# Tiles 10 and 11 of the second FFN layer as a seventh pair of seven block products, with the engines' lists laid out anew from batch 3's loads on

## The chip, the cores and the metric

The kernel runs on one core of a Trainium2 chip, which has five engines with an instruction list each: TensorE (PE, with its weight loads shown apart as PEld), VectorE (DVE), ScalarE (ACT), GpSimd (POOL) and SyncE (SP). They wait for each other through semaphores alone. The metric is the device time of one execution in microseconds, the median of several runs.

## The reference

Block-sorted attention for 4 batches of 8 heads (768 tokens, head size 64, blocks of 96 tokens), then a feed-forward network (FFN) over the 3072 tokens that come out. Cut to what matters:

```python
P = sinkhorn(sort_net, rounds=5)                  # 8x8 per batch and head
k_sorted = einsum('bhij,bhjcd->bhicd', P, k_b)    # and v_sorted alike
scores = q_b @ k_sorted.T / sqrt(64)              # within a block of 96
attn = softmax(scores); x = attn @ v_sorted       # x: 3072 tokens x 512
h = x @ w_in                                      # 512 x 2048
g = maximum(h, 0) + alpha * minimum(h, 0)
out = g @ w_out                                   # 2048 x 512
```

## The kernel before

**Stages.** One batch's attention and the FFN of the tokens that came out earlier run interleaved. A group g = 0..31 is one block of 96 tokens over 8 heads. For a group of batches 1 to 3, `attention` makes the scores on PE (line 761, into the PSUM tile psS), their negated maxima on DVE (767), eight exponentials on ACT (795), a transposing DMA on SP (800), the product with the sorted v on PE (815, into psO), a reciprocal and a scaling (823, 828, the latter on DVE or ACT), and a transpose into xT (a DMA at 843, or PE and a copy in batch 1). The next group's scores need psS free, which it is when the eight exponentials have read it. `conv_k`, `prep_k`, `conv_v` and `prep_v` sort k and v of the batch ahead: POOL copies (661, 411), PE products (674, 715), and a copy out of PSUM by ACT or DVE (411).

**FFN.** The tokens go in ten chunks, most of 384 tokens. For each of 16 slices of the hidden size `ffn1` makes four matmuls of 384 columns into one of two banks of psH (886), ACT takes the negated positive part (896), and DVE combines the two into hT (900). A psH bank is used again two slices later, so PE waits for line 900 when DVE is late. `ffn2` computes 128 tokens x 512 outputs as 16 matmuls of 512 columns in four groups of four (925), copies them out (411) and stores them (939). Tiles 12 to 23 go in six pairs instead, through `strassen`: the two tiles, each split by even and odd hidden slices, and w_out, split by the halves of its 512 outputs, are 2x2 blocks, and the product takes seven block products in place of eight (the Winograd form). A block product is eight matmuls of 256 columns in two groups of four (1024). It needs eight sums of hidden blocks per pair (999, on DVE or POOL, in the tile Sm or VDz), eight sums of weight blocks that are made once (`w_sums`, 963, in KS, VST and WT), three copies of a partial result to SBUF (`snap`, 1034, listed as line 411) and three additions on DVE on the way out (`total`, 1039).

**What sets the order.** Every piece of work is an entry of a graph, numbered as it is added, with its readers and writers. The table `SEQ` lists the numbers in one order for all engines; a letter behind a number names the engine where the work may run on several (p POOL, a ACT, d DVE). `arrange` splits it into one list for each engine and `emit` writes the lists with the waits that the data need. An engine works its list off in order, so an instruction that waits holds up all behind it. `PAIRS` names the pairs and which of two buffer sets each takes; set 0 is Sm and sn, set 1 VDz and KSz, which `conv_v` and `conv_k` use until batch 3 is sorted. For pairs below 12 the code at 973 and 1004 (`one`) puts all seven products into one PSUM bank, one half of psYP, in another order.

Of the kernel before, what the change touches and what calls it, by code (L numbers as in the profile page):

```python
# [57 lines left out]
712 743 716 736 725 713 720 804 663 717 707 664 721 665d 726 758 710 737 722 744 718 759 639 808 734 698 745
719 610 760 699 666 700d 749 708 735d 740 732 750 746 741 751 733 793 742 747 738 622 613 794 755 739 761 727
611 756 752 728 729d 701 781 768 753 757 795 754 782 805 730 767 775 769 803 776 778 770d 796 828 777 771 762  # L60
606 779 772 607 783 773 787 780 693 829 608 774 790 788 763 612 806 764d 789 797 791 765 807d 784 609 792 830
798 838 785d 810 836 813 811 831 856 837 822 799d 812 840 814 841 748 816 817 842 815 857 839 819 820 864 823
818 844 640 843 667 904p 865d 867 858 868 866 832 821 845 731 847 869d 824 833 846 870 850 848 851 849 853 825
834d 854 859 835 871d 890 852 905p 855 912p 702 826 891 913 872 881 873 882 914p 875 892 874 860 883 861 884
885 862d 887 876 948 888 886 889 898 800 915p 899 949 906p 863 901 900 877 902 878 903 916p 917p 945 942 950
922 946 943 893 968 908 910 947 951 879 959 944 956 969 918p 960 919p 961 957 958 920 921 894 923 965 895 896d
909p 924d 925 962 970 966 926 967 911p 786 897 963 964 988 979 976 971 952 928 880 927 980 989 766 981 977 827
990 907p 978 932d 985 982 929 933 1024p 991 983 953 1008 986 954d 972 984 996 997 987 999 1000 934 955 1009
801 930 973 998 974d 931 1022p 935 1001 1002 1010 992 936 1003 975 1030 937 993 1005 1023p 1031 994d 1004 1058
1034d 1006 938 1007 939 1059 995 1016 1019 1017 940 1018 1020 1036 1032 1021 1033 1052 1035 1011 1025p 1060  # L70
1055 1038 1026p 1027p 1053 1039 1056 1054 1057 1078 1079 1012 1066 1069 1037 1061 1067 1092p 1068 1040 1013
1070 1028p 1072 1071 1042d 1094p 1075 1073 1076 1043 941 1014d 1096p 1044 1097p 1062 1074 1041 1086 1077 1080
1089 1087 1015 1045d 1100 1063 1128 1064d 1029 1101 1090 1104 1088 1091 1122 1046 1125 1129 1065 1048 1093p
1123 1126 1106 1107 1124 1127 1098p 1049 1130 1050 1136 1112 1139 1137 1081 1154 1138 1102 1082 1113 1083 1103
1142 1140 1141 1155p 1114 1143 1105 1145 1146 1108 1144 1148 1156 1147 1109 1095p 1115d 1151 1110 1149 1150
1184 1162 1131 1152 1185 1163 1099 1153 1084d 1186 1188 1166 1157p 1187 1132 1111 1192 1168 1189 1193 1158
1190 1191 1196 1116 1197 1118 1194 1133 1159p 1195 1198 1134 1169 1199 1174d 1119 1161p 1216p 1200 1120 1201
1204 1205 1160 1164 1051 1085 1202 1135 1047 1232 1175 1217p 1165 1203 1206 1207 1176 1167 1208 1212 1177d
1170 1209 1171 1172 1210 1211 1246 1213 1214 1215 1250 1222p 1121 1247 1248 1173 1251 1249 1224 1218p 1225
1228 1252 1254 1255 1220p 1253 1117 1178 1256 1221p 1258 1257 1180 1230 1233 1259 1262 1263 1260 1261 1181  # L80
1266 1223p 1264 1265 1234 1267 1268 1231 1294 1278p 1269 1179 1270 1182 1271 1274 1280p 1286 1275 1272 1226
1227 1273 1276 1236 1235 1277 1279p 1287 1290 1183 1237 1295 1282 1283 1292 1284p 1229 1293 1281p 1238 1296
# [233 lines left out]
def bass_sinkhorn_attn__then__act_prelu_kernel(  # L316
# [634 lines left out]
    def w_sums():  # L951
        w = lambda ft, h: AP(w_out_bf, ft * DM + h * 256, [[FT_TILES * DM, 128], [2 * DM, 4], [1, 256]])
        old = [("KS", 0)], [("VST", 0)] + [("VST", 0, x) for x in range(4)]
        for n, x, y, op in ((1, (0, 1), (0, 0), AluOpType.subtract), (3, (1, 1), (0, 1), AluOpType.subtract),
                            (2, (1, 1), 1, AluOpType.subtract), (4, (1, 0), 2, AluOpType.subtract)):
            for hf in range(2):
                def f(e, n=n, x=x, y=y, hf=hf, op=op):
                    def at(v):
                        if isinstance(v, tuple):
                            return w(8 * hf + v[0], v[1])  # L960
                        t, ld, off = wt(v, 4 * hf)
                        return AP(t, off, [[ld, 128], [256, 4], [1, 256]])
                    return e.tensor_tensor(out=at(n), in0=at(x), in1=at(y), op=op)
# [156 lines left out]
    for t0, t1_, _ in CHUNKS:  # L1120
# [18 lines left out]
    for g in range(NG + 12):  # L1139
        while fp < len(ffn_plan) and ffn_plan[fp][0] < g:  # L1140
# [100 lines left out]
```

## Time and profile before

| | |
|---|---|
| median of 3 runs | 231.47 us (231.02 to 232.26) |
| profiled execution | 231.12 us |
| its span, first to last instruction | 229.4 us |
| TensorE clock granted | 1.000 |
| busy, of the span | PE 95%, DVE 80%, ACT 68%, POOL 68% |

The span is 1.72 us shorter than the time of its execution. Busy shares are means over the whole span, and what decides is which engine the others wait for in the stretch that the change touches. That stretch begins at about 97 us, and its core lies between 107 and 155 us, where tiles 10 and 11 are computed.

### The profile page before, as it was taken

What the parts mean: (1) busy time and instruction counts of PE and PEld (TensorE: products, weight loads), DVE (VectorE), ACT (ScalarE), POOL (GpSimd) and SP (SyncE); (2) the same over time, 40 slices, a digit from 0 to 9 for tenths busy, and PEclk for the clock granted to TensorE, in tenths of its full rate; (3) what the DMA queues carried; (4) which work ended last, traced back from release to release, by engine and by line L of the source; (5) the groups of instructions that cost most, each with busy time, mean ns of one, the idle gap of its engine ahead of it and who ended that gap; (6) DMA issues with size and microseconds to landing.
All of it is one profiled execution on the core that took longest, in us unless ns stands there. A gap on an engine that the chain in (4) does not pass through costs nothing.

```text
span 229.4 us, 6744 instructions
## 1 busy us (share of the span) xinstructions
PE 218.5 (95%) x2717; PEld 151.6 (66%) x2735; DVE 183.2 (80%) x390; ACT 155.4 (68%) x424; POOL 156.8 (68%) x185
## 2 busy tenths in 40 slices
PE   3899999999999999999999999999999999999994
PEld 3457588695556655565565566556777777999983
DVE  5669599896898979777678798899897887886583
ACT  4479667889989595857898787777666673554310
POOL 7969129849075995872989979579965945448760
PEclk9999999999999999999999999999999999999999
DMA  5999999995994499599949998533764223041104
GB/s 64 215 211 202 218 204 190 179 170 91 181 174 86 52 124 115 109 101 251 175 103 110 167 134 153 87 69 91 165 132 82 73 54 80 20 148 49 52 0 184
DMA packets 64031, 29.03 MB, mean 127 GB/s; under 512 B 55280, under 2 KB 58880, under 8 KB 64000
## 3 DMA queue, kind: packets, MB, share of 16 engines
q0 software_dynamic: 24816, 13.63, 46.7%
q1 hardware_dynamic: 39184, 14.97, 32.8%
q8 instruction: 21, 0.34, 0.6%
q14 instruction: 10, 0.08, 0.1%
HBM read 27.28 MB, written 6.29 MB: 146 GB/s over the span
## 4 chain that ended last, share of the span: by engine, by line
PE 75%; DMA 10%; POOL 9%; DVE 3%; issue 1%; ACT 0%; POOLq 0%
PE psH L886 33%; PE psYP L925 16%; PE psYP L1024 12%; DMA KS<-in_k_dram 10%; POOL KSz L661 3%; PE psS L761 3%; PE psO L815 3%; PE psYP L715 3%; PE psO L1024 2%; PE psYP L674 2%; POOL w_in_bf L1102 1%; DVE hT L900 1%; DVE Sm L999 1%; POOL QN L441 1%; PE psS L1024 1%
## 5 line engine op out<-in xcount | busy, mean ns | idle before, releaser
L886 PE MATMUL psH<-xT,w_in_bf 128*128 128x384 bf16 (+1 forms) x624 | 97.3, 295 | 0.5 <-DVE hT L900 0.4
L900 DVE SCALAR_TENSOR_TENSOR hT<-t,omaT,psH 128x384 bf16<-128x384 f32 (+1 forms) x156 | 79.0, 529 | 17.6 <-ACT t L896 16.2
L896 ACT ACTIVATE t<-psH 128x384 f32<-128x384 f32 x126 | 61.2, 495 | 39.5 <-PE psH L886 38.8
L886 PEld LDWEIGHTS psH<-xT,w_in_bf 128*128 128x128 bf16 x624 | 54.5, 98 | 22.1 <-DVE hT L900 1.3
L795 ACT ACTIVATE Esb<-psS,nf 96x96 bf16<-96x96 f32 x192 | 46.1, 344 | 1.1 <-DVE nf L767 1.1
L925 PE MATMUL psYP<-w_out_bf,hT 128*128 128x512 bf16 x174 | 44.8, 379 | 1.3 <-issue 0.5
L411 POOL COPY VDz<-VST 64x384 bf16<-64x384 bf16 x40 | 33.9, 846 | 17.5 <-PE psYP L715 13.1
L661 POOL COPY KSz<-KS 64x512 bf16<-64x512 bf16 x36 | 22.1, 613 | 15.1 <-DMA KS<-in_k_dram 9.0
L925 PEld LDWEIGHTS psYP<-w_out_bf,hT 128*128 128x128 bf16 x192 | 16.9, 98 | 15.4
L767 DVE TENSOR_REDUCE nf<-psS 96x8 f32<-96x768 f32 x24 | 22.8, 948 | 4.3 <-PE psS L761 4.3
L999 POOL TENSOR_TENSOR VDz<-hT 128x512 bf16<-128x512 bf16 x12 | 14.2, 1184 | 9.1 <-DVE hT L900 6.2
L828 DVE TENSOR_TENSOR xq<-psO,rec 96x512 bf16<-96x512 f32 x29 | 19.8, 683 | 0.6
L441 POOL DMA_DIRECT2D QN<-in_q_dram x24 | 20.1, 852 | 0.1
L815 PEld LDWEIGHTS psO<-VS,ET 112*128 112x128 bf16 x248 | 11.0, 98 | 2.7 <-ACT xT L411 0.5
L815 PE MATMUL psO<-VS,ET 112*128 112x65 bf16 x248 | 12.7, 194 | 0.0
L999 POOL TENSOR_TENSOR Sm<-hT 128x512 bf16<-128x512 bf16 x7 | 8.1, 1154 | 6.4 <-DVE hT L900 5.6
L761 PEld LDWEIGHTS psS<-KT,QTz 64*128 64x128 bf16 (+1 forms) x248 | 6.4, 97 | 8.2 <-ACT t L896 3.4
L999 POOL TENSOR_TENSOR Sm<-Sm,hT 128x512 bf16<-128x512 bf16 x5 | 5.8, 1154 | 8.5 <-DVE Sm L999 8.2
L1024 PE MATMUL psYP<-w_out_bf,hT 128*128 128x256 bf16 x80 | 11.2, 273 | 0.0
L761 PE MATMUL psS<-KT,QTz 64*128 64x96 bf16 (+1 forms) x248 | 10.8, 206 | 0.4 <-DVE KT L411 0.4
L411 ACT ACTIVATE VS<-psYP 112x512 bf16<-112x512 f32 x13 | 9.0, 692 | 3.1 <-PE psYP L715 2.8
L411 DVE CAST VS<-psYP 112x512 bf16<-112x512 f32 x13 | 9.0, 690 | 1.8 <-PE psYP L715 1.8
(196 smaller groups left out, 329.3 us busy)
## 6 DMA issues: line engine op xcount, KB each, us to landing
out_dram<-outstg SPq DMA_DIRECT2D x24, 256.0 KB, 2.4
KS<-in_k_dram POOLq DMA_DIRECT2D x3, 768.0 KB, 9.6
QN<-in_q_dram POOLq DMA_DIRECT2D x24, 96.0 KB, 4.9
w_in_bf<-in_moe_w_in_dram POOLq DMA_DIRECT2D x4, 512.0 KB, 18.8
w_out_bf<-in_moe_w_out_dram POOLq DMA_DIRECT2D x2, 1024.0 KB, 19.8
VST<-in_v_dram POOLq DMA_DIRECT2D x4, 384.0 KB, 11.3
hT<-in_q_dram POOLq DMA_DIRECT2D x1, 768.0 KB, 7.3
VST<-in_v_dram POOLq DMA_DIRECT2D x1, 768.0 KB, 13.3
```

Source lines behind the costliest of these rows:

```text
L411: return e.activation(o, i, ACTF.Copy) if e is nc.scalar else e.tensor_copy(o, i)
L661: G.add(POOL, lambda e, hp=hp: e.tensor_copy(AP(KSz, hp * 64 * 3072 + u % 3 * 1024 + hp * 64, [[3072, 64], [128, 8], [1, 64]]), AP(KS[n], ...
L761: inst = e.matmul(o, AP(QTz[n], hp * 64 * 3072 + h4 * 768 + i * 96, [[3072, 64], [1, w]]), AP(KT[n], hp * 64 * ld + (h4 * 8 + i) * bk, [[l ...
L767: G.add(DVE, lambda e: e.tensor_reduce(AP(nx, 0, [[8, 96], [4, 2], [1, 4]]), AP(psX, 0, [[1024, 96], [512, 2], [96, 4], [1, 96]]), AxisLis ...
L795: inst = e.activation(AP(Esb[me], p * 128, [[1024, 96], [64, 2], [1, 48]]), AP(psX, (p // 4) * 512 + (p % 4) * 96, [[1024, 96], [48, 2], [ ...
L815: inst = e.matmul(AP(psZ, hp * 512 + h4 * 68, [[1024, 128], [1, 65]]), AP(ET[me] if far else ET[m], pos(h4, hp) * 96, [[800, nk], [1, 128] ...
L886: inst = e.matmul(AP(pt, poff + x * n, [[1024, 128], [1, n]]), AP(w_in_bf, kt * DFF + (ft + x) * 128, [[KT_TILES * DFF, 128], [1, 128]]), ...
L896: G.add(ACT, lambda e: e.activation(AP(t1, tb, [[1152, 128], [1, k * n]]), AP(pt, poff, [[1024, 128], [1, k * n]]), ACTF.Relu, scale=-1.0) ...
L900: G.add(DVE, lambda e, x=x: e.scalar_tensor_tensor(out=AP(hT, (ft + x) * RING + place(tok), [[FT_TILES * RING, 128], [1, n]]), in0=AP(t1, ...
L925: inst = e.matmul(AP(bank[0], bank[1], [[1024, 128], [1, n]]), AP(hT, ft * RING + place(tok), [[FT_TILES * RING, 128], [1, 128]]), AP(w_ou ...
L999: return e.tensor_tensor(out=sv(n, hf), in0=i[0], in1=i[1], op=op)
L1024: inst = e.matmul(AP(pt, po + off, [[1024, 128], [1, 256]]), sa, mb, start=begin and j == 0, stop=j == 7, skip_group_check=True)
```

## The change

`PAIRS` gains the entry 10, so that tiles 10 and 11 go through `strassen` with buffer set 0 and one PSUM bank. Since the smallest pair is now 10, the weight sums are added to the graph ahead of it, and all later numbers shift. `SEQ` is new from entry 626 on. No other line differs.

```diff
@@ SEQ @@
-626 591 593 556 627 594 600 557 620 625 595 602 628 629 601 621 558d 489 598 596 630 647 597d 599 509 631 559
+626 591 489 625 594 556 627 593 629 595 557 630 558d 628 631 596 620 559 600 597 509 365 560 601 632 621 633
...
-    PAIRS = {12: 1, 14: 0, 16: 1, 18: 0, 20: 1, 22: 0}
+    PAIRS = {10: 0, 12: 1, 14: 0, 16: 1, 18: 0, 20: 1, 22: 0}
```

Counted over the lists, PE loses 32 matmuls of 512 columns and gains 56 of 256. The sums of hidden blocks go from 10 on DVE and 38 on POOL to 20 and 36, and the sums of weight blocks from 2 on DVE and 6 on POOL to 6 and 2. DVE also gains three additions of line 1039 and loses four copies into KT, which ACT takes; ACT gains three copies into sn and one scaling of line 834.

**TensorE, where tiles 10 and 11 end.** Names: psH is written by the first layer, psYP by the second, psS by the scores, psO by attention's second product. Before:

```order
L925 MATMUL psYP<-w_out_bf,hT 128x512 x4
L761 MATMUL psS<-KT,QTz 128x96 x8
L886 MATMUL psH<-xT,w_in_bf 128x384 x8
L925 MATMUL psYP<-w_out_bf,hT 128x512 x4
L815 MATMUL psO<-VS,ET 128x65 x8
L886 MATMUL psH<-xT,w_in_bf 128x384 x8
L925 MATMUL psYP<-w_out_bf,hT 128x512 x4
L761 MATMUL psS<-KT,QTz 128x96 x8
L886 MATMUL psH<-xT,w_in_bf 128x384 x8
L925 MATMUL psYP<-w_out_bf,hT 128x512 x8
```

The same place now:

```order
L761 MATMUL psS<-KT,QTz 128x96 x8
L886 MATMUL psH<-xT,w_in_bf 128x384 x4
L815 MATMUL psO<-VS,ET 128x65 x8
L1024 MATMUL psYP<-VST,Sm 128x256 x8
L886 MATMUL psH<-xT,w_in_bf 128x384 x8
L1024 MATMUL psYP<-WT,Sm 128x256 x4
L761 MATMUL psS<-KT,QTz 128x96 x8
L1024 MATMUL psYP<-WT,Sm 128x256 x4
L886 MATMUL psH<-xT,w_in_bf 128x384 x4
L1024 MATMUL psYP<-w_out_bf,hT 128x256 x12
```

Groups of 512 columns have become groups of 256 that read the sums in Sm, WT and VST, and two score products (line 761) that follow each other have less work between them.

**VectorE, in the middle of the chunk of tokens 1536 to 1919.** hT is the first layer's result, KT the sorted k, nf the negated maxima, rec and xq the scaling of attention. Before:

```order
L900 SCALAR_TENSOR_TENSOR hT<-t,omaT,psH 128x384
L411 CAST KT<-psYP 128x32x2x8
L823 RECIPROCAL rec<-psO 96x8
L900 SCALAR_TENSOR_TENSOR hT<-t,omaT,psH 128x384 x2
L828 TENSOR_TENSOR xq<-psO,rec 96x512
L411 CAST KT<-psYP 128x32x2x8
L900 SCALAR_TENSOR_TENSOR hT<-t,omaT,psH 128x384 x2
L767 TENSOR_REDUCE nf<-psS 96x8
L999 TENSOR_TENSOR VDz<-VDz,hT 128x512
```

The same place now:

```order
L900 SCALAR_TENSOR_TENSOR hT<-t,omaT,psH 128x384 x2
L963 TENSOR_TENSOR VST<-w_out_bf,KS 128x1024
L900 SCALAR_TENSOR_TENSOR hT<-t,omaT,psH 128x384
L999 TENSOR_TENSOR Sm<-Sm,hT 128x512
L823 RECIPROCAL rec<-psO 96x8
L900 SCALAR_TENSOR_TENSOR hT<-t,omaT,psH 128x384
L828 TENSOR_TENSOR xq<-psO,rec 96x512
L900 SCALAR_TENSOR_TENSOR hT<-t,omaT,psH 128x384
L999 TENSOR_TENSOR Sm<-hT 128x512
L767 TENSOR_REDUCE nf<-psS 96x8
```

The copies into KT have gone to ACT, and a weight sum and two hidden sums stand between the first layer's combinations, the last of them ahead of a reduction that the exponentials wait for.

**GpSimd, at batch 3's loads.** VST and KS receive v and k, VDz and KSz their reordered copies. Before:

```order
L475 DMA VST<-in_v_dram 64x1536
L459 DMA KS<-in_k_dram 128x768
L475 DMA VST<-in_v_dram 64x1536 x3
L459 DMA KS<-in_k_dram 128x768 x3
L411 COPY VDz<-VST 64x8x48 x6
L661 COPY KSz<-KS 64x8x64
L411 COPY VDz<-VST 64x8x48 x2
```

The same place now:

```order
L475 DMA VST<-in_v_dram 64x1536 x4
L963 TENSOR_TENSOR KS<-w_out_bf 128x1024
L459 DMA KS<-in_k_dram 128x768 x4
L411 COPY VDz<-VST 64x8x48 x10
L661 COPY KSz<-KS 64x8x64
L411 COPY VDz<-VST 64x8x48 x4
```

A weight sum now stands between the loads of v and those of k, and ten copies of v, where there were six, come before the first copy of k.

More of the change, by code (lines that the diff above doesn't have):

```diff
@@ L53 @@
 522d 528 531 618 577 579 532 561 580 584 523 533 614 524 562d 567 623 615 565 616 619 592 566 164 624 568 590
-626 591 593 556 627 594 600 557 620 625 595 602 628 629 601 621 558d 489 598 596 630 647 597d 599 509 631 559
-632 365 560d 641 633 603 585 642 644 604 586 587d 648 645 643 634 588 649 589d 646 605 653 635 656 654 659 655
-657 650 551 658 676 660 651 668 679 677 688 678 680 669 661 681 689 703 674 682 672 662 694 683 670 685 695
-690 459 686 671 675d 696 636 687 691 802 637 684 704 714 638d 652 692 697 705 673 723 706 711 724 715 809 709
@@ L58 @@
[L58 to L82, printed above, removed]
@@ L83 @@
-1239d 1219p 1297 1298 1285 1299 1240 1300 1288 1301 1302 1242 1289 1291 1243 1241 1244 1303 1304 1305 1306
-1245 1307
+626 591 489 625 594 556 627 593 629 595 557 630 558d 628 631 596 620 559 600 597 509 365 560 601 632 621 633
+641 585 644 642 634 645 586 587d 647 824 588 635 648 589d 599 598 659 822p 643 653 646 656 654 603 660 604 649
+657 605 655 676 661 662 602 658 669 668 677 679 650 459 670 825 680 651 636 678 694 695 682 672 681 671 683
+684 674 688 637 685 696 689 697 711 707 723 673 686 675d 703 638d 705 708 687 714 663 712 704 706 805 690 715
@@ new lines @@
+709 724 732 713 725 664 691 716 717 758 710 733 737 692 826 720 734 665d 639 759 830 743 718 726 551 721 698
+744 719 740 768 722 699 760 793 735d 738 761 749 700d 804 745 802 741 739 736 750 794 727 767 742 769 701 752
+795 751 728 753 729d 755 746 756 666 770d 754 762 730 796 771 860 775 772 757 763 823 778 747 776 610 861 773
+779 862 781 777 780 764d 613 765 787 774d 611 790 788 782 803 888 831 806 789 791 606 807 810 792 652 813 622
+834 811 797 863 814 783 889 607 812 608 890 868 612 816 609 815 809 870 808 874 817 869d 819 693 891 820 798
@@ new lines @@
+872 784 873 871 799d 818 821 827 875 876 896 879 785 877 838 897 878 835 900 898 899 880 864 640 901 828p 882
+667 832p 902 865 881 866d 839 800 883 903 885 884 916 840 904 892 841 886 842 905 930p 931p 836 917 887 907
+918 906 893 867 843d 908 894d 702 910 844 966 911 845 846 909 967 913 940 914 912 847 829 748 848 968 924 919
+915 927 928 895 925 986 849 969 987 850 920 921 929 926 932p 851 837p 852 853 988 854 963 960 833p 933p 731
+964 989 922d 965 961 856 934p 935p 1006 857 936p 962 977 978 858 974 937p 970 975 1007 938 976 939 971 979
@@ new lines @@
+1008 942 941 980 981 983 1026 972d 982 944 984 985 855 990 1027 991 945 994 923 950 997 951 943 995 766 801
+952 973 946 998 996 1000 999 992 953d 1001 1003 947 1042p 1004 1009 993 1028 1048 1010 1002 1014 1005 948 1017
+1110p 786 1011 1076 1015 1012d 1049 1029 949 1016 1018 1040p 1019 1020 954 1023 956 1021 859 1052d 1022 1024
+957 1041p 1034 1025 1037 1013 955 958 1077 1035 1050 1051 1036 1054 1053 1070 1030 1038 1039 1078 1044 1071
+1073 1096 1045 1055 1056 1046p 1043p 1072 1074 1075 1112p 1031 1060 1032d 1084 1085 1087 1057 1061 1097 1088
@@ new lines @@
+1098 1089 1079 1062 1086 1111p 1058 1099 1093 1063d 1090 1080 1094 1146 1095 1047p 1091 1118 1092 1107 1104
+1116p 1147 1059 1108 1105 1109 1119 1143 1106 1140 1122d 1081 1114p 1064 1124 959 1082d 1083 1066 1067 1148
+1115p 1141 1144 1142 1068 1125 1154 1100 1145 1113p 1157 1033 1155 1101 1120 1172 1130 1158 1156 1117p 1121
+1160 1159 1163 1173 1149 1131 1123 1126 1161 1162 1164 1166 1167 1127 1132 1165 1168 1169 1202 1133d 1102d
+1170 1171 1203 1128 1129 1206 1180 1134 1150 1181 1207 1136 1204 1176 1137 1184 1205 1178p 1174p 1103 1208
@@ new lines @@
+1210 1211 1177p 1209 1214 1069 1138 1186 1187 1175 1212 1182 1151 1213 1215 1216 1217 1152 1218 1183 1192d
+1219 1193 1220 1221 1222 1223 1185 1224 1194 1195 1226 1225 1250 1227 1188 1153 1228 1065 1230 1242 1189 1231
+1229 1232 1264 1233 1190 1268 1265 1269 1266 1267 1270 1234p 1243 1191 1271 1235p 1272 1251 1179p 1273 1276
+1139 1277 1196 1238p 1274 1198 1275 1199 1278 1252 1280 1279 1284 1281 1236 1296 1306 1239p 1304 1282 1246
+1285 1240p 1200 1248 1283 1286 1287 1237 1249 1288 1289 1292 1244 1241p 1253 1293 1290 1294 1295 1312 1135
@@ L85 @@
+1197 1291 1305 1297 1300 1301 1254 1255 1313 1314 1298 1308 1310 1311 1302 1316 1201 1256 1303 1307 1317 1299p
+1257d 1318 1315 1258 1245 1260 1319d 1320 1259 1321 1247 1261 1262 1322 1323 1263 1309 1324 1325
 """.split()
```

## Prediction

> **What bounds the kernel now.** I read the busy shares first (the table above), then a table of the engines' busy time by stretch, then TensorE's groups and the timeline of the few places where TensorE waits.
>
> In the stretch table the columns are start and end, length, busy time of PE, PEld, DVE, ACT and POOL with the number of instructions, clock, DMA share and GB/s:
>
> ```profile
> 106.80:119.00 12.20, 11.99 (x116) 7.01 (x118) 8.60 (x14) 10.15 (x33) 9.50 (x13) 1.00 0.83 168
> 119.00:133.00 14.00, 13.73 (x149) 8.06 (x150) 11.60 (x21) 11.20 (x32) 13.43 (x18) 1.00 1.01 134
> 133.00:144.00 11.00, 10.79 (x120) 6.75 (x121) 9.89 (x19) 8.30 (x26) 9.34 (x10) 1.00 1.44 128
> 144.00:155.50 11.50, 11.27 (x89) 6.00 (x88) 10.53 (x18) 8.83 (x27) 7.47 (x6) 1.00 0.44 79
> 130.00:140.00 10.00, 9.79 (x118) 6.14 (x115) 9.02 (x17) 8.04 (x23) 8.65 (x11) 1.00 1.69 153
> 150.00:160.00 10.00, 9.82 (x83) 6.14 (x76) 9.66 (x16) 7.63 (x25) 8.06 (x6) 1.00 0.34 76
> ```
>
> The first four rows are the stretch of the change, 106.8 to 155.5 us. TensorE is busy 47.78 of its 48.7 us, and part of what is missing is records that the trace lost. VectorE is second with 40.62 (83%), GpSimd has 39.74 (82%), ScalarE 38.48. TensorE's groups from 100 us to the end say what it waited for (last columns: busy time, mean ns of one, idle before and its cause):
>
> ```profile
> L886 PE MATMUL psH<-xT,w_in_bf 128*128 128x384 bf16 (+1 forms) x396 | 63.4, 300 | 0.2 <-DVE hT L900 0.2
> L925 PE MATMUL psYP<-w_out_bf,hT 128*128 128x512 bf16 x87 | 22.5, 379 | 0.8 <-issue 0.5
> ```
>
> The 0.8 before line 925 is put down to "issue", that is, to lost records. The only real waits after 100 us are these two:
>
> ```profile
> 155.46 1.47 PE L886 MATMUL psH<-xT,w_in_bf 128*128 128x384 bf16 x8 [0.18 <-DVE hT L900]
> 220.97 0.61 PE L1024 MATMUL psS<-VST,Sm 128*128 128x256 bf16 x4 [0.35 <-DVE Sm L999]
> ```
>
> So TensorE is the bound and has almost no slack: time leaves the kernel only with TensorE's own work, or with these 0.53 us. The first wait tells where the next bound is: it falls in the window 150 to 160 us, where VectorE was busy 9.66 of 10 us. In 130 to 140 us, with 9.02 of 10, TensorE did not wait. Somewhere between 90 and 97% VectorE begins to hold TensorE up.
>
> **TensorE's saving.** From the chain of work (start, duration, instructions):
>
> ```profile
> 103.71 0.86 PE psYP L925 x4
> ...
> 200.04 1.31 PE psYP L1024 x12
> ```
>
> A group of four matmuls of 512 columns takes 0.86 us; tiles 10 and 11 have eight such groups, 6.88 us. Twelve matmuls of 256 columns take 1.31, so 0.109 each; 56 of them take 6.10. The saving is 6.88 - 6.10 = **0.78 us**, all on the path.
>
> **VectorE's additions.** The durations, from its timeline and groups:
>
> ```profile
> 142.73 0.68 DVE L828 TENSOR_TENSOR xq<-psO,rec 96x512 bf16<-96x512 f32 x1
> 143.33 0.68 DVE L411 CAST KT<-psYP 128x512 bf16<-128x512 f32 x1
> 146.09 0.41 DVE L999 TENSOR_TENSOR VDz<-VDz,hT 128x512 bf16<-128x512 bf16 x1
> 152.63 0.68 DVE L963 TENSOR_TENSOR VST<-w_out_bf,KS 128x1024 bf16<-128x1024 bf16 x1
> 153.35 1.53 DVE L963 TENSOR_TENSOR KS<-w_out_bf,VST 128x1024 bf16<-128x1024 bf16 x1
> 226.42 0.42 DVE L1039 TENSOR_TENSOR outstg<-psO,sn 128x256 f32<-128x256 f32 x1 [0.45 <-PE psO L1024]
> ```
>
> ```profile
> L823 DVE RECIPROCAL rec<-psO 96x8 f32<-96x8 f32 x17 | 3.4, 199 | 1.1 <-PE psO L815 1.0
> L411 DVE COPY sn<-psYP 128x256 f32<-128x256 f32 x5 | 2.1, 420 | 0.1
> L1039 DVE TENSOR_TENSOR outstg<-psYP,sn 128x512 f32<-128x512 f32 x2 | 1.4, 684 | 0.0
> L411 DVE COPY outstg<-psYP 128x512 f32<-128x512 f32 x1 | 0.6, 636 | 0.0
> ```
>
> In the stretch VectorE gets five weight sums of 0.68 in place of two that took 0.68 and 1.53 (+1.19), four more hidden sums of 0.41 (+1.64), additions of 0.42 and 0.68 (+1.10), a copy into sn (+0.42), a reciprocal and a scaling (+0.20 +0.68) and a copy into VS, priced like KT's (+0.68). It loses three copies into KT (-2.04) and one output copy (-0.64). That is +3.2. Neighbouring records overlap by 0.08 (142.73 + 0.68 ends after 143.33), so nine more instructions take 0.7 less: +2.5, and VectorE stands at 40.6 + 2.5 = 43.1 of 48.7, 88%. By that alone nothing new waits.
>
> **Waits between VectorE and GpSimd.** The sums read two SBUF tiles, and their durations differ. Beside the rows above stand these:
>
> ```profile
> 218.46 1.15 DVE L999 TENSOR_TENSOR Sm<-hT 128x512 bf16<-128x512 bf16 x1
> 222.39 0.42 DVE L999 TENSOR_TENSOR Sm<-hT,Sm 128x512 bf16<-128x512 bf16 x1
> ...
> 152.79 1.53 POOL L999 TENSOR_TENSOR VDz<-hT 128x512 bf16<-128x512 bf16 x1 [1.63 <-DVE hT L900]
> 218.18 1.15 POOL L999 TENSOR_TENSOR Sm<-hT 128x512 bf16<-128x512 bf16 x1 [1.12 <-DVE hT L900]
> ```
>
> The sum at 218.46 began beside a GpSimd sum that ran to 219.33 and ended 0.28 behind it; alone, at 146.09 and 222.39, it takes 0.41. The weight sum took 0.68 alone and 1.53 beside a GpSimd sum that ran to 154.32. So a VectorE sum waits until GpSimd's instruction is over. Whether GpSimd's copies block it too the trace shows in one place only, a small VectorE product of two SBUF tiles (its group's row has least, median and greatest duration in ns), the later of the two beside copies:
>
> ```profile
> L621 DVE TENSOR_TENSOR BDV<-mkhV,dsel x2: 311/427/543, 45.4 to 96.9; 128x64 bf16<-128x64 f32 x2
> 96.94 0.54 DVE L621 TENSOR_TENSOR BDV<-mkhV,dsel 128x64 bf16<-128x64 f32 x1
> 96.80 1.95 POOL L661 COPY KSz<-KS 64x512 bf16<-64x512 bf16 x3 [0.58 <-PE psYP L674]
> L411 POOL COPY VDz<-VST 64x384 bf16<-64x384 bf16 x40 | 33.9, 846 | 17.5 <-PE psYP L715 13.1
> ```
>
> The earlier one takes 0.31, the one beside the copies 0.54, so I let copies block as sums do. If VectorE's and GpSimd's new lists run at the pace of the old rows, ten of VectorE's sums in the stretch meet work of GpSimd: six its copies (0.85 each), four its sums (1.15). The wait for one is bounded by 0 and by 1.53 - 0.68 = 0.85. I take what a start at a random moment gives: half an instruction, (6 x 0.42 + 4 x 0.58) / 10 = 0.48, in GpSimd's busy share of 0.82, so 0.40 each and 4.0 in all. VectorE then has 47.1 of 48.7, 97%. The old window with that share cost TensorE 0.18 in 10 us; over 48.7 us that is **0.9 us** of new waits before line 886, in place of the old 0.18, which lies inside them.
>
> [...]
>
> **Costed at nothing.** On GpSimd a weight sum moves ahead of the loads of batch 3's k, and four more copies of v ahead of its first copy:
>
> ```profile
> L963 POOL TENSOR_TENSOR KS<-w_out_bf 128x1024 bf16<-128x1024 bf16 x2 | 4.2, 2118 | 0.2
> 105.45 0.53 POOL L459 DMA_DIRECT2D KS<-in_k_dram  x1 [1.77 <-DVE xT L411]
> 113.91 0.61 POOL L661 COPY KSz<-KS 64x512 bf16<-64x512 bf16 x1
> 132.94 0.40 PE L674 MATMUL psYP<-BDM,KSz 128*128 128x64 bf16 x8
> ```
>
> The loads of k come up to 2.1 us later, but before the change their issue waited 1.8 us for xT at the last of them, and the first copy of k began only at 113.91, behind six copies of v. Four more (4 x 0.85) put it at 117.3, and TensorE's first product with it came at 132.94: 15 us are cover enough. Without them TensorE would stand for up to those 3.4 us. ScalarE, which takes four copies into KT, three into sn and one scaling, stands at 79%. At the end six VectorE sums of the last pair now follow each other with one GpSimd sum beside them, so the wait at 220.97 goes: between 0 and **0.35 us**, and I take all of it, since 222.39 shows 0.42 for such a sum.
>
> **Sum.** 231.12 - 0.78 - 0.35 + 0.9 = 230.9 for an execution like the profiled one. The median is 0.35 above that execution (231.47), so **231.2 us**. Its own range goes from 230.7 (half of the new waits) to 231.9 (the wait at the end stays, the new ones come to 1.3).
>
> **Rivals.** *TensorE stays dense*: no sum but those beside GpSimd's sums waits, and the old 0.18 goes too. 231.12 - 0.78 - 0.35 - 0.18 = 229.8, so 230.2 on the median. [...] Against: so little slack in VectorE that one crowded spot is enough.
>
> *VectorE becomes the bound* (the slower side): if the ten sums wait longer than (48.7 - 43.1) / 10 = 0.56 us each, VectorE needs more than the stretch has, and TensorE waits before line 886 for all that is over. At the full 0.85 it needs 51.6, 2.9 too much: 231.12 - 0.78 - 0.35 + 2.9 = 232.9, so 233.2. For it: the one wait measured on a weight sum is the full 0.85, and five such sums now lie in the stretch. Against: the weight sum right ahead of it, at 152.63, did not wait at all.
>
> *The scores become the bound.*
>
> ```profile
> 116.31 0.95 DVE L767 TENSOR_REDUCE nf<-psS 96x8 f32<-96x768 f32 x1 [0.65 <-PE psS L761]
> 117.44 1.92 ACT L795 ACTIVATE Esb<-psS,nf 96x96 bf16<-96x96 f32 x8
> 119.60 0.34 PE L761 MATMUL psS<-KT,QTz 64*128 64x96 bf16 x8
> L815 PE MATMUL psO<-VS,ET 112*128 112x65 bf16 x248 | 12.7, 194 | 0.0
> ```
>
> From the end of one group's scores (116.3) to the start of the next (119.60) the maxima and exponentials need 3.3 us. In the order now, the work between two score products is in one place twelve matmuls of line 886 (63.4 / 396 = 0.16 each), twelve of line 1024 and eight of line 815 (12.7 / 248 each): 1.92 + 1.31 + 0.41 = 3.6. The slack is 0.3, and a maximum that stands behind a blocked sum (0.85) overruns it by about 0.5. Three such places, at 0.4 each, add 1.2 to the forecast: 232.4. Against: the maximum must stand behind a blocked sum in all three places.
>
> **How the numbers follow.** Forecast 0.50, dense 0.20, VectorE the bound 0.22, scores 0.08. The range leaves out about a tenth at either end: 230.1 (the dense case, where half of it lies below) to 233.3 (just past VectorE's case). Half a per cent, 1.16 us, is about what a measurement of this kernel can tell from no change. Faster by more (below 230.3): 0.11 of the dense case and 0.01 of the forecast's tail, 0.12. Slower by more (above 232.6): 0.20 of VectorE's case, 0.04 of the scores', 0.03 of the forecast's, 0.27. The rest, 0.61, is within.
>
> **What would show it.** TensorE's line 925 has 32 matmuls fewer and line 1024 56 more at 0.109. Between 107 and 155 us idle time before line 886, put down to VectorE's hT, adds up to about 0.9. VectorE's sums show a spread of durations, near 0.41 and 0.68 where GpSimd rests and up to 0.85 more beside its copies; if they are short beside copies, the dense case holds. The wait near 220 us is gone. Idle time before line 761 put down to exponentials shows the scores' case. The forecast is wrong if GpSimd's copies, not VectorE's sums, do the waiting and the sorted k comes late, which line 761 would show as waits for KT.

## The result, and the profile after

| | before | after |
|---|---|---|
| median of 6 executions | 231.62 us (231.02 to 232.31) | 240.89 us (238.86 to 242.40) |
| ratio | | 1.0388, 95% interval 1.0336 to 1.0439 |
| profiled execution, its span | 231.12, 229.4 us | 240.92, 239.1 us |
| TensorE clock granted, mean | 1.000 | 0.992 |
| busy, of the span | PE 95%, DVE 80%, ACT 68%, POOL 68% | PE 93%, DVE 79%, ACT 66%, POOL 62% |

The changed kernel is 3.9% slower. The forecast said 231.2 us, and its range ended at 233.3. In this document a ratio leaves out executions that took over 1.5% longer than the fastest of the same kernel.

First the timeline of TensorE in the profile after, all instructions from 90 us on that waited over 0.16 us (before, there were two: 0.18 at 155.46 and 0.35 at 220.97):

```profile
115.41 0.42 PE L815 MATMUL psO<-VS,ET 112*128 112x65 bf16 x8 [4.78 <-DMA ET<-Esb]
150.33 0.82 PE L886 MATMUL psH<-xT,w_in_bf 128*128 128x384 bf16 x4 [0.68 <-DVE hT L900]
153.83 1.47 PE L886 MATMUL psH<-xT,w_in_bf 128*128 128x384 bf16 x8 [0.42 <-DVE hT L900]
159.77 0.82 PE L886 MATMUL psH<-xT,w_in_bf 128*128 128x384 bf16 x4 [0.61 <-DVE hT L900]
186.38 0.61 PE L1024 MATMUL psYP<-VST,Sm 128*128 128x256 bf16 x4 [0.53 <-DVE Sm L999]
```

Half of the loss is one wait, for something that the forecast does not name: attention's second product (line 815) of group 16 waits for the DMA that transposes the group's exponentials into ET. Before the change the same product came later and did not wait; the row from before, and the issues of the transpose before and after (the second is a row of two issues, whose start is the first one's):

```profile
113.80 0.41 PE L815 MATMUL psO<-VS,ET 112*128 112x65 bf16 x8
106.08 1.22 SPq L800 DMA_TRANSPOSE ET<-Esb  x1
105.50 5.70 SPq L800 DMA_TRANSPOSE ET<-Esb  x2
```

What follows the wait is in the table of stretches (columns as in the prediction, the third from the end is TensorE's clock):

```profile
111.00:115.40 4.40, 0.00 (x0) 0.00 (x0) 0.00 (x0) 0.27 (x1) 2.44 (x3) 1.00 1.31 127
116.00:117.00 1.00, 1.00 (x11) 0.48 (x6) 0.69 (x1) 0.00 (x0) 0.00 (x0) 0.50 0.11 24
117.00:118.00 1.00, 1.00 (x12) 0.70 (x10) 0.78 (x2) 0.31 (x1) 0.00 (x0) 0.50 0.00 0
118.00:119.00 1.00, 1.00 (x5) 0.33 (x3) 0.78 (x3) 1.00 (x6) 0.78 (x1) 0.50 0.00 0
119.00:120.00 1.00, 1.00 (x6) 0.52 (x5) 1.00 (x2) 1.00 (x5) 0.89 (x2) 0.90 0.00 0
```

TensorE and VectorE stand still and ScalarE nearly so (0.27 of 4.40 us), while the DMA engines are busy (share 1.31). When TensorE starts again its granted clock is 0.50 for three us, 116 to 119, and 1.7 us of work are lost in that (0.5 in each of three rows, and 0.2 in all at the edges, with 0.83 from 115.4 to 116 and 0.90 from 119 to 120).

The other four waits are VectorE's sums beside GpSimd's instructions. VectorE's timeline, and below it GpSimd's at the same moments:

```profile
139.00 0.57 DVE L999 TENSOR_TENSOR Sm<-Sm,hT 128x512 bf16<-128x512 bf16 x1
147.62 2.06 DVE L999 TENSOR_TENSOR Sm<-Sm,hT 128x512 bf16<-128x512 bf16 x1
151.33 1.05 DVE L999 TENSOR_TENSOR Sm<-hT 128x512 bf16<-128x512 bf16 x1
157.54 1.65 DVE L963 TENSOR_TENSOR VST<-w_out_bf,VST 128x1024 bf16<-128x1024 bf16 x1
185.07 1.26 DVE L999 TENSOR_TENSOR Sm<-Sm,hT 128x512 bf16<-128x512 bf16 x1
```

```profile
138.44 0.85 POOL L661 COPY KSz<-KS 64x512 bf16<-64x512 bf16 x1
147.28 2.12 POOL L963 TENSOR_TENSOR KS<-w_out_bf,VST 128x1024 bf16<-128x1024 bf16 x1
150.77 1.32 POOL L999 TENSOR_TENSOR VDz<-hT 128x512 bf16<-128x512 bf16 x1
157.16 1.48 POOL L999 TENSOR_TENSOR VDz<-hT,VDz 128x512 bf16<-128x512 bf16 x1
184.75 1.30 POOL L999 TENSOR_TENSOR Sm<-hT,Sm 128x512 bf16<-128x512 bf16 x1
```

Each hidden sum ends 0.28 us after GpSimd's instruction beside it (147.62 + 2.06 = 149.68 against 149.40), and the weight sum 0.55 after. The long ones delay a combination of line 900 that stands behind them, or TensorE directly: 147.62 makes the wait at 150.33, 151.33 that at 153.83, 157.54 that at 159.77, 185.07 that at 186.38.

The sum of the two profiled executions: 240.92 - 231.12 = 9.80. The product of group 13, ahead of everything that changed, starts at 92.86 before and 93.80 after, so 0.94 is the executions' own difference at the start. The wait of line 815 is 4.78, the lost clock 1.7, the four waits 2.24, and the two waits of before (0.53) and the block products (0.78) are saved: 0.94 + 4.78 + 1.7 + 2.24 - 0.53 - 0.78 = 8.35. Of the remaining 1.45, about 0.8 is what the steps around these five waits took beyond wait and work (0.16 each: at 815 it is 5.16 us from the start of the matmul ahead to that of the product, 4.78 of it the wait, and such a matmul's own step is 0.22), 0.1 lies outside the span, 0.15 is a shorter wait at 231.07, and 0.4 is in small pieces that were not followed.

### The profile page after: what moved, and what is told of

Same layout as the page of the kernel before. It is cut to its first block, busy times and chain, and to the rows that moved or that the text cites. A ratio compares the mean times of both kernels' runs of the same rounds, so it can differ in the third digit from the quotient of the medians.

```text
span 239.1 us, 6831 instructions
## 1 busy us (share of the span) xinstructions
PE 222.2 (93%) x2759; PEld 154.4 (65%) x2759; DVE 189.1 (79%) x401; ACT 158.3 (66%) x438; POOL 147.3 (62%) x179
## 4 chain that ended last, share of the span: by engine, by line
PE 72%; DVE 11%; DMA 7%; ACT 6%; issue 1%; POOLq 0%
PE psH L886 29%; PE psYP L925 13%; PE psYP L1024 12%; DVE hT L900 5%; DMA ET<-Esb 4%; DMA hT<-in_q_dram 3%; DVE Sm L999 3%; PE psO L815 3%; PE psS L761 3%; PE psYP L715 3%; ACT Esb L795 2%; PE psO L1024 1%; PE psYP L674 1%; PE psYP L1198 1%; ACT t L896 1%
## 5 line engine op out<-in xcount | busy, mean ns | idle before, releaser
L886 PE MATMUL psH<-xT,w_in_bf 128*128 128x384 bf16 (+1 forms) x624 | 98.5, 297 | 2.1 <-DVE hT L900 2.0
L411 POOL COPY VDz<-VST 64x384 bf16<-64x384 bf16 x40 | 34.7, 867 | 22.5 <-PE psYP L715 18.7
L925 PE MATMUL psYP<-w_out_bf,hT 128*128 128x512 bf16 x160 | 41.1, 384 | 0.0
L925 PEld LDWEIGHTS psYP<-w_out_bf,hT 128*128 128x128 bf16 x160 | 14.1, 99 | 12.5 <-issue 0.6
L999 POOL TENSOR_TENSOR VDz<-hT 128x512 bf16<-128x512 bf16 x11 | 12.9, 1174 | 13.4 <-DVE hT L900 9.7
L828 DVE TENSOR_TENSOR xq<-psO,rec 96x512 bf16<-96x512 f32 x28 | 19.1, 682 | 0.5
L999 POOL TENSOR_TENSOR Sm<-hT 128x512 bf16<-128x512 bf16 x6 | 7.0, 1165 | 16.5 <-DVE hT L900 16.3
L1024 PE MATMUL psYP<-w_out_bf,hT 128*128 128x256 bf16 x96 | 13.4, 273 | 0.0
L999 POOL TENSOR_TENSOR Sm<-hT,Sm 128x512 bf16<-128x512 bf16 x6 | 7.2, 1196 | 7.2 <-DVE Sm L999 6.8
L761 PE MATMUL psS<-KT,QTz 64*128 64x96 bf16 (+1 forms) x248 | 10.9, 208 | 0.1
L411 ACT ACTIVATE KT<-psYP 128x512 bf16<-128x512 f32 x15 | 9.0, 597 | 3.0 <-PE psYP L674 2.9
```

The source lines that it names most:

```text
L411: return e.activation(o, i, ACTF.Copy) if e is nc.scalar else e.tensor_copy(o, i)
L761: inst = e.matmul(o, AP(QTz[n], hp * 64 * 3072 + h4 * 768 + i * 96, [[3072, 64], [1, w]]), AP(KT[n], hp * 64 * ld + (h4 * 8 + i) * bk, [[l ...
L886: inst = e.matmul(AP(pt, poff + x * n, [[1024, 128], [1, n]]), AP(w_in_bf, kt * DFF + (ft + x) * 128, [[KT_TILES * DFF, 128], [1, 128]]), ...
L925: inst = e.matmul(AP(bank[0], bank[1], [[1024, 128], [1, n]]), AP(hT, ft * RING + place(tok), [[FT_TILES * RING, 128], [1, 128]]), AP(w_ou ...
L999: return e.tensor_tensor(out=sv(n, hf), in0=i[0], in1=i[1], op=op)
L1024: inst = e.matmul(AP(pt, po + off, [[1024, 128], [1, 256]]), sa, mb, start=begin and j == 0, stop=j == 7, skip_group_check=True)
```

## The experiments

The entry numbers of the diffs: 822 is GpSimd's weight sum in front of the loads of k, 602 to 605 are those loads (602 is number 0), 636 to 638 are group 16's second product, reciprocal and scaling. All runs are timed beside the kernel before, whose median was 231.75 to 232.19 in them.

### Which of the two moves makes the wait at 115 us

Two things were moved against each other. The transpose is issued when the exponentials are done: at 106.08 us before, with the product at 113.80, and at 105.50 after, with TensorE ready for the product at 110.63. And the loads of k are issued later. Below, the transpose's issue and the DMAs issued around it, in the profile after (a row gives issues, KB, median us from issue to landing), and under it before:

```profile
KS<-in_k_dram POOLq DMA_DIRECT2D x3, 192.0 KB, 8.6
ET<-Esb SPq DMA_TRANSPOSE x1, 9.9
```

```profile
KS<-in_k_dram POOLq DMA_DIRECT2D x1, 192.0 KB, 6.1
ET<-Esb SPq DMA_TRANSPOSE x1, 6.2
```

**e1_sum_behind_k_loads**

```diff
-659 822p 643
+659 643
...
-602 658
+602 822p 658
```

> The changed kernel with one edit: GpSimd's weight sum that stood in front of the four loads of k stands behind them. Queue theory (the transposing DMA of group 16's exponentials, issued at 105.5 us, lands only when the loads of k beside it have landed, and TensorE's second product of that group waits for it): the loads are issued 2.1 us earlier, the transpose lands at about 113.3 instead of 115.4, TensorE's wait of 4.8 us before line 815 shrinks to about 2.7, and the time falls from 240.9 to between 237.5 and 239. Rival (ports: VectorE's weight sums and GpSimd's copies slow the DMAs, wherever the loads stand): the wait stays between 4.3 and 5.3 and the time at 240.5 to 241.5.

Four executions took 235.8, 236.3, 242.5 and 243.6 us (the last two with a clock of 0.985 and 0.979); the ratio, 1.0174 (1.0132 to 1.0217), is that of the two short ones. In the profiled one, 242.5, the wait was 5.46 us, the transpose took 10.6, and the clock was 0.5 in the slice from 113.8 to 119.8 us. So there the wait did not shrink, and the expectation failed: the first two loads went out at 102.60 in place of 103.88, but the last two still stood behind the load that waits for xT of group 15, and were issued from 105.44 on. The two short executions, with clocks of 0.997 and 1.000, took about 5 us less than the changed kernel. They have no profile, so this run alone does not tell what the sum's place is worth; e3 below does.

**e2_product_later**

```diff
-651 636 678
+651 678
...
-688 637 685
+688 685
...
-711 707
+711 636 707
...
-703 638d 705
+703 705
...
-687 714
+687 637 638d 714
```

> The changed kernel with one edit: TensorE's second product of group 16 stands seven entries later (behind three slices of the first layer, two groups of the second, the next scores and a product of v, about 4.4 us of work), VectorE's reciprocal and scaling of that group likewise; the loads stay. Queue theory: the transpose still lands at about 115.4, but TensorE has work until 115, so the wait is 0.3 to 0.8 instead of 4.8, and the clock stays at 1.0 behind it (it was 0.5 for three us); the time falls by 4.2 + 1.7 to about 235. Rival (the wait only marks time that VectorE's added work costs anyhow): waits before line 886 or 761 grow by the same amount, and the time stays above 239.

236.41 us (ratio 1.0199, 1.0146 to 1.0252). In the profiled execution, 235.42, the transpose took 10.6 us, landing at 115.4, TensorE waited 0.98 and the clock stayed at 1.00. Waits of 2.25 us before lines 886 and 1024 remained as they were, and one of 0.30 came at 132. Between the profiled executions 5.5 us are gained (240.92 - 235.42), which is the stall less what was left of it, and its clock (4.78 - 0.98 + 1.7); between the medians it is 4.5.

**e3_both**, the two edits together:

> Both edits of the two runs before. Queue theory: no wait before line 815 and no fall of the clock; 240.9 - 4.95 - 1.7 = 234.2 us. What remains above 230.3 then comes from TensorE's four waits for VectorE between 147 and 187 us (2.2 us in the changed kernel). Rival (VectorE's added work costs it anyhow): above 237.

236.21 us (1.0180, 1.0150 to 1.0211), two us more than forecast: the transpose took 10.9, a wait of 1.28 was left, and one of 0.82 stood at 133. Beside e2 (236.41, 10.6 and 0.98) the sum's place gained nothing.

**e5_k_loads_late**

```diff
-654 603 660
+654 660
...
-660 604 649
+660 649
...
-657 605 655
+657 655
...
-662 602 658
+662 658
...
-672 681
+672 603 604 605 602 681
```

> The changed kernel with one edit: the four loads of k stand behind six copies of v on GpSimd, and so are issued at about 113 instead of 104 to 107 us; product and weight sums stay where they are. Queue theory: beside the transpose only the loads of v are under way, which land by about 108.7, so it lands by about 109.5, TensorE does not wait before line 815 and the clock stays at 1.0; about 234.2 us, if k's first copy at 122 us is still in time. Rival (ports, or the transpose's own place behind other transposes): it lands as late as before and the wait stays near 4.8.

235.22 us (1.0125, 1.0065 to 1.0186). The transpose of group 16, in the same place and with the same sums around it, landed after

```profile
DMA to landing us min/median/max: 2.8/2.8/2.8
```

and TensorE did not wait at line 815, as the queue theory said. The loads went out at 110.2 to 112.4 instead, and there another transpose, of q, kept TensorE waiting for 1.06 us at 119.9. So it is the loads of k beside the transpose that make it late, 2.8 against 9.9 us here.

**e9_before_product_early**, on the kernel before:

```diff
-650 551
+650 636 551
...
-696 636 687
+696 687
```

> The kernel before the change with one edit: TensorE's second product of group 16 stands where the change put it, behind the last group of tile 6 in the second layer, five groups of work earlier; loads as before. Theory A: TensorE comes to it at 108.2, the transpose lands at 112.3, so a wait of about 4.1 us before line 815 and a clock of 0.5 for about three us behind it: 231.8 + 4.1 + 1.5 = 237.4, most of what the change lost, without any of its block products. Rival (the change's own work makes the stall): no wait, 231.8 to 232.5.

237.18 us (1.0240, 1.0205 to 1.0275). TensorE waited 3.30 us before line 815, with a clock of 0.50 from 112.6 to 115.6:

```profile
111.64 0.42 PE L815 MATMUL psO<-VS,ET 112*128 112x65 bf16 x8 [3.30 <-DMA ET<-Esb]
112.60:113.60 1.00, 1.00 (x4) 0.46 (x3) 0.16 (x1) 0.49 (x1) 0.94 (x2) 0.50 0.07 16
```

One moved product, with no block product and no new sum, costs 5.4 us of the 9.3.

**e4_before_k_load_last**, also on the kernel before:

```diff
-595 602 628
+595 628
...
-605 653
+605 602 653
```

> The kernel before the change with one edit: k's load number 0 stands last of the four. Theory A: the transpose of group 16, issued at about 106 us, lands at about 115.5 instead of 112.3; TensorE comes to its product at 113.8, so a wait of about 1.7 us before line 815 where there was none, and no fall of the clock; 231.8 + 1.7 = 233.5. Theory B (the load's place does not matter): no wait, 231.8.

231.56 us (0.9994, 0.9977 to 1.0012). The transpose took 6.9 us, not the 9.4 that theory A asked for, landed at 113.5, and the product at 114.32 did not wait. The load's place alone costs nothing while the product stands late.

**e7_first_k_load_early**, on the changed kernel:

```diff
-600 597
+600 602 597
...
-662 602 658
+662 658
```

> The changed kernel with one edit: k's load number 0, which waits for nothing at that time and stood last of the four, behind the one that waits for xT of group 15, stands second again, behind the first load of v, as before the change. The weight sum in front of the other three loads and the early product stay. Theory A (the transpose of group 16 lands when the load bytes around it are through, and one load of four issued at 106 instead of 99 us makes it some 3 us later): it lands at 111.5 to 112.5, as before the change, the wait before line 815 falls from 4.8 to between 0.9 and 1.9, the clock stays at 1.0; 240.9 - 3.4 - 1.7 = about 236. Theory B (the weight sum in front of the loads is what delays them): no change, a wait of 4 us or more and 240 to 242.

237.93 us (1.0246, 1.0192 to 1.0300). In the profiled execution, 236.85, the transpose took 7.6, the wait was 2.49, and the clock stayed at 1.00 behind it; two of the four took 239.0 and 242.2 with clocks of 0.99. The gain has the sign of theory A; the wait is 0.6 us above its range, and the median 2 us above its 236, with the clock down in two of the executions.

**e11_weight_sums_away**, on e7, with the first three weight sums later:

```diff
-647 824 588
+647 588
...
-659 822p 643
+659 643
...
-670 825 680
+670 680
...
-717 758
+717 822p 824 825 758
```

> The run e7 (the changed kernel with k's load number 0 second) with the first three weight sums, one on GpSimd and two on VectorE, some 15 us later, so that none runs while the loads are under way; the product stays early. Queue theory (the transpose of group 16 lands late since load bytes share the DMA engines with it, whatever computes meanwhile): it takes 7 to 10 us from issue to landing as in e7 (7.6) and e8 (9.3), TensorE waits 2 to 5 us before line 815, and the time is 237 to 241. Port theory (sums on VectorE and GpSimd slow the loads' descriptors, and so the transpose): 5 to 6.5 us to landing as in the kernel before (6.2), a wait under 1.5 us, 235 to 236.

241.57 us (1.0387, 1.0323 to 1.0452). In the profiled execution, 243.86, the longest of the four, there was no sum on VectorE or GpSimd near the transpose, and still it took 8.3 us, TensorE waited 3.24, and its matmuls from 113.3 to 119 us took nearly twice their time (four of line 886 1.46 and 1.49 in place of 0.81), with a mean clock of 0.986. So the port theory does not hold for that execution, and no run shows a port; the other three executions, 239.9 to 242.8, lie above its 236 too, but have no profile. Some of the time belongs to the moved sums themselves: waits of 1.25 and 1.41 us came at 128 and 141.

**e12_before_transpose_early**, on the kernel before:

```diff
-642 644
+642 634 644
...
-643 634 588
+643 588
```

> The kernel before with one edit: ScalarE makes group 16's exponentials ahead of one slice of the first layer, as the change has it, so that the transposing DMA is issued at about 105.1 instead of 106.1 us, just ahead of the last load of k instead of just behind it. If a transpose ahead of a load is overtaken by it (the changed orders, all ahead of one or two loads, took 7.6 to 10.9 us; those behind them 5.3 to 6.9): 7.5 us or more to landing, at 112.6 or later, a wait of 0 to 1.5 us before line 815 and 231.8 to 233.3. If only the bytes count that are under way at its issue: lands at 112.3 as before, no wait, 231.8.

231.89 us (1.0003, 0.9988 to 1.0018). Issued at 105.36, ahead of the last load at 105.62, the transpose took 7.9 us, against 6.2 behind it; it landed at 113.3, one us later than in the profile before, and was still in time.

Set side by side, by how many loads of k were issued after the transpose:

| loads issued after it | us from issue to landing |
|---|---|
| none near it (e5) | 2.8 |
| none, the last just before it (before, e9) | 6.2, 5.3 |
| one beside it or after it (e4, e7, e12, e11, and e8, e10, e13, e14, e15 below) | 6.9, 7.6, 7.9, 8.3, and 9.1 to 9.3 |
| two (after, e1, e2, e3) | 9.9, 10.6, 10.6, 10.9 |

The transpose did not keep its place in these runs: with one load issued behind it on another queue it took 0.7 to 4.0 us more than with the last load just before it, with two 3.7 to 5.6 more. These are single profiled executions; only e12 changes the order alone (7.9 against 6.2), the other runs also change how close together the loads are. In what way a later load makes the transpose late, no run shows.

### The waits for VectorE's sums

**e8_loads_as_before_product_later**, the edits of e7 and e2 and this one:

```diff
-659 822p 643
+659 643
...
-605 655
+605 822p 655
```

> The changed kernel with the three edits together: k's load number 0 second, the weight sum behind all loads, the product of group 16 seven entries later. Theory A: the transpose lands at 112 to 112.5, TensorE comes to the product at about 114.5, no wait there and none of 0.3 to 1.0 before line 886 at 132; what is left are the four waits for VectorE's blocked sums (2.2 us): 231.8 - 0.7 + 2.2 = 233.3. Rival (VectorE's added work costs more than the four waits): above 235.

235.35 us (1.0149, 1.0120 to 1.0178), two us above theory A and just inside the rival's 235. No wait at line 815 was left (the transpose landed at 115.2, three us later than theory A said, and TensorE came at 115.35), and the clock was 1.00. TensorE's only waits from 95 us on were the four of the changed kernel, at 144, 148, 154 and 180 us (0.69, 0.42, 0.61, 0.54), with the same sums of 2.06, 1.05 and 1.65 us on VectorE. A part of what lies between this and the forecast is told in the last section.

**e10_blocked_sums_moved**, on e8 (835 and 836 are pair 10's hidden sums, 829 a weight sum):

```diff
-878 835 900
+878 900
...
-899 880
+899 835p 880
...
-832p 902
+832p 836p 902
...
-931p 836 917
+931p 917
...
-847 829 748
+847 748
...
-926 932p
+926 829 932p
```

> The run e8 (loads as before, product later) with VectorE's three sums moved that waited beside GpSimd's between 147 and 160 us: the two hidden sums of pair 10 go to GpSimd, ahead of its weight sum and behind its own first sum, and the weight sum into VST stands on VectorE some five instructions later, when GpSimd has nothing left. Lock theory (each of TensorE's waits before line 886 there is a VectorE sum that stood until GpSimd's instruction was over): the waits of 0.69, 0.42 and 0.61 us go, together with what lay beside them 2.2 us, so 235.35 - 2.2 = 233.2. Rival (VectorE is simply full there, 95% and more): the waits shift by an instruction or two, and the time stays within 0.6 of 235.35.

236.32 us (1.0178, 1.0132 to 1.0224); the edit missed its aim. The three waits before line 886 were gone, but 829 now came too late for a block product:

```profile
155.20 0.61 PE L1024 MATMUL psYP<-VST,hT 128*128 128x256 bf16 x4 [1.99 <-DVE VST L963]
156.00:157.00 1.00, 1.00 (x7) 0.67 (x6) 0.00 (x0) 0.00 (x0) 0.92 (x2) 0.50 0.34 61
```

and the clock fell to 0.50 behind this wait too. Three of the four executions had a mean clock of 0.991 to 0.993, and the fourth, at 1.000, was the shortest (235.09).

**e13_sums_moved_in_time**, on e10:

```diff
-827 875
+827 829 875
...
-926 829 932p
+926 932p
```

> As e10, but the weight sum into VST stands early on VectorE, right behind the sum that it reads, so that TensorE's product has it in time (in e10 it came 2.0 us late). Lock theory: no wait over 0.3 us before line 886 or 1024 between 140 and 165 us, and the time is 235.35 - 2.2 = 233.2, between 232.6 and 234.0. Rival (VectorE is full there): new waits before line 886 of 1 us or more in all, 234.5 or more. Below 231.8 it would beat the kernel before; the waits left at 180 and 225 us (0.5 and 0.3) speak against that.

232.88 us (1.0043, 1.0028 to 1.0058). No wait of TensorE was left between 132 and 178 us; its sums on VectorE in that stretch took

```profile
139.98 0.70 DVE L963 TENSOR_TENSOR VST<-w_out_bf,KS 128x1024 bf16<-128x1024 bf16 x1
140.72 0.98 DVE L963 TENSOR_TENSOR VST<-w_out_bf,VST 128x1024 bf16<-128x1024 bf16 x1
```

and GpSimd does the two others. Three moved sums are worth 2.5 us. Two of them also left VectorE (0.41 each), so this run by itself does not part their place from VectorE's load; the part on why the prediction was wrong has a stretch of 94% without a wait. One wait was left in front of it:

```profile
131.87 1.46 PE L886 MATMUL psH<-xT,w_in_bf 128*128 128x384 bf16 x8 [1.25 <-DVE xq L828]
```

The scaling of the last group that this slice reads had been done at 126.0, so the releaser named is not the one; of the three transposes into xT that SyncE issues one behind the other from 124.5 us, beside the loads of q, the last was issued at 127.1 and landed 4.7 us later, at 131.8.

**e14_xT_of_group17_earlier**, on e13 (666 is the transpose of group 17 into xT):

```diff
-726 551
+726 666 551
...
-756 666 770d
+756 770d
```

> As e13, but SyncE issues the transpose of group 17's output into xT two transposes earlier, so that the three into xT no longer stand one behind the other at 124.5 to 128.3 us, and the last of them, which the first slice of tokens 1536 waits for, is issued about one us earlier. Block-product theory (without waits the seventh pair is worth its 0.78 us): the wait of 1.25 us at 131.9 shrinks to 0 to 0.5 and the time to 231.7 to 232.2. Rival (the wait comes from q's loads beside the transpose, whatever the order on SyncE): it stays at 0.9 or more, 232.6 or more.

232.36 us, against 232.19 of the kernel before beside it: 1.0001 (0.9981 to 1.0022). The wait at 131.9 is gone; the only one left from 95 us on is 0.54 at 177. It is a draw, though the time outside the span took a part of it back (last section).

**e15_and_q_loads_later**, on e14 (606 to 613 are the loads of q, which go behind 808, a copy of k; only the first of the eight old places is shown):

```diff
-776 610 861
+776 861
...
-808 874
+808 610 613 611 606 607 608 612 609 874
```

> As e14, and GpSimd issues the eight loads of batch 3's q behind two more copies of k, about 8 us later, so that none is under way beside those transposes. Block-product theory with both causes taken away: no wait at 131.9, and 231.79 - 0.78 + 0.5 (the waits left at 178 and 222 us beyond those of before) = 231.5, between 231.2 and 232.0. Rival (the loads then meet the next transposes or the turned q comes late): new waits before line 815, 761 or 886 at 140 to 155 us, above 232.5.

238.49 us (1.0278, 1.0251 to 1.0304). The rival's side, but mainly not by a transpose (a wait of 0.42 for the turned q came at 149.65): the eight issues hold GpSimd itself, and the copies of k behind them come late.

```profile
135.89 6.62 POOL L441 DMA_DIRECT2D QN<-in_q_dram  x8
143.85 0.61 PE L674 MATMUL psYP<-BDM,KSz 128*128 128x64 bf16 x8 [3.71 <-POOL KSz L661]
```

## Why the prediction was wrong

**The bound** was read rightly: TensorE is dense, and of the 9.80 us between the two profiled executions its waits (4.78 + 2.24) and its clock (1.7) make 8.72.

**The step that failed** is the part "Costed at nothing". It says that the loads of k "come up to 2.1 us later" and asks only who reads k, 15 us later. Who else is on the DMA engines while they run was not asked, and TensorE's product of group 16 was not followed at all: the change moves it ahead of the next scores and of five more groups of work, from 7.7 us behind the issue of its transpose to 5.1. Before, a transpose of 6.2 us had 1.5 us to spare; now one of 5.3 to 10.9 us has none. e9 shows the moved product alone to cost 5.4 us, e5 that it costs nothing at line 815 when the loads are elsewhere, and e4, e12 and before that the loads cost nothing there while the product is late. It takes an early product and loads beside its transpose; of the change's two moves the product's alone is enough. The term that the sum lacked is 4.78 + 1.7 us.

**The saving** of 0.78 is seen in its larger part. In e14 TensorE needs 125.25 us from the start of group 16's scores to the end of its last matmul, before 124.67; a group of 0.86 that stood ahead of those scores before stands behind them in the new order, so like for like it is 0.28 us less. The waits over 0.1 us in it are 0.54, 0.15 and 0.13, before 0.18 and 0.35, so without waits it is 0.57 less, in one execution of each. Why not the whole 0.78, no run shows.

**VectorE against GpSimd**: that a VectorE sum ends only behind GpSimd's instruction beside it was right (by 0.28 us for the hidden sums, 0.55 for the weight sum), the size of what it costs was not. The forecast gave ten sums 0.40 each and turned 97% of VectorE into 0.9 us. In fact beside copies a sum lost next to nothing (0.16 at 139.00), since there the copy often was the one to wait (the copies of v at 108.78, 124.32 and 127.22 took 1.30, 1.19 and 0.99 in place of 0.85). Beside sums the four of the timeline above lost 0.64 to 1.65 and a fifth, at 229.76, lost 0.85; two of them are above the bound of 0.85, which knew no GpSimd instruction longer than a hidden sum though the weight sums of 2.12 stood in a row of their own. TensorE lost 0.68 + 0.42 + 0.61 in the stretch, where the forecast had 0.9, and 0.53 behind it, 2.24 in all. The way from one to the other was wrong too: it is not the share of VectorE that counts. From 126 to 140 us VectorE was busy 94% and TensorE did not wait, and from 155 to 165, where it waited 0.61, VectorE had 88%:

```profile
126.00:140.00 14.00, 13.91 (x148) 7.99 (x142) 13.19 (x24) 12.03 (x38) 12.20 (x16) 1.00 1.15 129
155.00:165.00 10.00, 9.39 (x95) 6.55 (x94) 8.79 (x15) 7.33 (x25) 5.34 (x5) 1.00 0.40 89
```

The blocked sums cost TensorE time where a combination that it waits for, or TensorE itself, came right behind them: 0.68, 0.42, 0.61 and 0.53 us behind the four of the timeline. In the rows looked at here whichever of the two instructions began first held the other up, and it goes both ways: the sum at 147.62, begun 0.34 us after GpSimd's of 2.12, took 2.06 in place of 0.41 and ended 0.28 behind it; the copy at 108.78, begun 0.08 after a weight sum of 0.68, took 1.30 in place of 0.85. That is no wait for a semaphore: it lies within the instructions' own durations.

**The end**: the wait at 220.97 went, as forecast; what took its place is 0.15 us at 231.07.

**The rivals**: the scores never became the bound and the sorted k did not come late (idle before line 761 is 0.1 us in all), and VectorE's case had the right sign with the wrong place. No rival had a DMA in it. The profile had the sign: transposes beside the loads took 6.2 and alone 2.8 to 3.0 already before the change.

## What to carry to other kernels

When an order is laid out anew, follow each moved consumer back to its producer, and where that is a DMA compare the new distance with the longest landing that the trace shows next to the traffic of that place, not with the usual one. Here a transpose on one queue took 2.8 us with no load near, 5.3 and 6.2 with the last load just before it, and 6.9 to 10.9 with loads issued beside or after it on another queue; keep bulk loads away from short transposes that are waited for, or give the consumer several us. And place sums with two SBUF inputs where the other of the two engines pauses: three such sums cost 2.5 us in one place (e8 against e13), TensorE waited for none of them once they had another place or the other engine, and busy shares didn't tell which (VectorE's 94% without a wait, 88% with one of 0.61).

## What had not been expected

**The clock after a stall.** TensorE's granted clock fell to 0.50 for about three us around the end of a wait of 4.78 (after), 3.30 (e9), 3.71 (e15) and also 1.99 us (e10), and for six around one of 5.46 (e1, by the slice of its page) or 3.24 (e11, by its matmuls' durations); it stayed at 1.00 behind one of 2.49 us (e7, profiled execution) or 1.28 (e3). Where it fell, the stall cost another 1.5 to 1.7 us (after, e9, e10, e15), in e11 about 3. The length of the wait alone does not tell when: 1.99 us brought the drop and 2.49 did not, and the same kernel had a lower mean clock in some executions than in others (e7: 0.992 and 0.991 in the two long ones, 0.998 and 1.000 in the two short; e10: 0.991 to 0.993 in three, 1.000 in the shortest). What decides it, no run shows.

**Time outside the span.** In the kernel before and its variants (e4, e9, e12) the execution was 1.67 to 1.80 us longer than its span in every run. In the changed kernel and its variants it was 1.67 to 2.93, with medians up to 2.5 (e14, e8). In e14 the median span is 230.0 us and before, beside it, 230.5, so the span is shorter by 0.5 while the time is not. e8's two us above its forecast hold 0.7 of this. What happens there no profile shows, and it stays open.
